# A linear-attention block with Strassen products: KV sums and numerators in PE array tiles, later exps, a third Strassen value pair

## Chip, cores, metric

One core of one Trainium2 chip. The metric is the time of one execution in microseconds (us) on the device, the median of several; smaller is better. All outputs were compared with the reference and were correct. All runs here are fast runs with a granted clock of 0.998 to 1.0.

## The reference, cut

```python
h  = x + A(layernorm(x))            # linear attention, 32 heads of 32
h2 = h + B(layernorm(h))            # gated feed-forward, F = 3584
# A, with S = 2048, D = 1024:
q, k, v = split_heads(x @ wqkv)
phi = lambda t: where(t > 0, t + 1, exp(t)) + 1e-6
kv  = einsum("bhsd,bhse->bhde", phi(k), v);  z = phi(k).sum(over s)
num = einsum("bhqd,bhde->bhqe", phi(q), kv)
den = einsum("bhqd,bhd->bhq", phi(q), z) + 1e-6
return (num / den) @ wo
```

Everything is bf16. The sum `z` is had by a column of ones beside `v`, the denominator by a column of `z` beside `kv`.

## The kernel before

The kernel writes each engine's instructions in a fixed order; every engine works through its own list in order, and a semaphore wait stands only where two engines meet. So *where in the program* an instruction stands decides what it blocks. The parts that matter (cuts marked):

**A Strassen group** makes a 2x2 block product from seven products of four 128x512 matmuls each. A product adds up in a *bank*, one of the eight 128x512 parts of the accumulator `ps`; a bank must be read out before another product takes it. They keep Strassen-like names but run in the order P1, P7, P6, P2, P5, P4, P3. In this text "the second product" means P2, and so on. After each, `hook(i)` runs work queued for that place. The exps of two of a group's four blocks are queued in this way: they are *deferred* into the next group.

```python
a = alloc_bank(pool); f = alloc_bank(pool); b = alloc_bank(pool)
prod(a, X(0,0), W(0,0), True, "P1")
ident_act(bank(b), bank(a), ...)          # "fk1": ACT copies the partial sum; P6 adds onto it
hook(1)
prod(f, SX(2), TW(2), True, "P7")         # SX, TW: operand sums made by DVE
ident_act(s7, bank(f), ...)
hook(2)
c = alloc_bank(pool)
prod(b, SX(1), TW(1), False, "P6")
ident_act(bank(c), bank(b), ...)          # "fk2": P5 adds onto it
hook(3)
prod(a, X(1,0), W(1,0), False, "P2");  # ... evacuate block 11 (for k and q: exp, min/add, max = phi)
hook(4)
prod(c, SX(0), TW(0), False, "P5")
ident_act(sc, bank(c), ...)               # "sc": must be read before P3 adds onto bank c
s22 = e22(bank(f), ..., sc, ...); s22[0]()    # DVE add, frees bank f
hook(5)
prod(b, X(1,1), TW(3), False, "P4")
s21 = e21(bank(b), ..., s7, ...); s21[0]()    # DVE add, frees bank b
hook(6)
prod(c, SX(3), W(1,1), False, "P3")
# ... what is left of the evacuation runs in the NEXT group's hooks:
pend[1] = s12
pend[2] = list(s22[1:])                   # exp on ACT, then two DVE operations
pend[3] = list(s21[1:])
hook(7)
```

**The order of groups**: eight plain value pieces of 8 matmuls, then key group 0, then four more plain value pieces (the third pair, row blocks 4 and 5), then key group 1, value group 3, key group 2, value group 4 and so on to key group 7; eight query groups (r = 0, 1; ct = 0 to 3); then the output projection, interleaved with the numerators; then the feed-forward part.

**KV sums and numerators**, one 128x128 product for four heads of which only the four diagonal 32x32 blocks are wanted:

```python
def kvacc(st):                            # 8 matmuls; bursts of two row blocks = 16
    for g in range(NG):                   # g: group of four heads, three PSUM banks
        mm(kv_out(g), pa[:, g*P:(g+1)*P], vv[:, sv, g, 0:P+1], first, ...)
# once: DVE multiplies by a block mask into kvz (5 operations)
def a2_num(st):                           # 8 matmuls, two per bank
    for g in range(NG):
        mm(ps[:, NB[g//2], (g%2)*256 : ...+P+HPG], pqT[:, r, t, g, i*P:(i+1)*P], kvz[:, g, 0:P+HPG], True, True, ...)
```

Five banks serve the groups (`P1_POOL = [3..7]`), four in the second row of query groups (`A_POOL[1] = [4..7]`).

Of the kernel before, what the change touches and what calls it, by code (L numbers as in the profile page):

```python
# [132 lines left out]
def bass_sequential_preLN__linear_attn_block__glu_gated_reglu__prompt_kernel(  # L133
# [17 lines left out]
    H = 32  # L151
# [20 lines left out]
    VW = P + 2  # L172
    KZW = P + HPG
    GPB = 3
    GPN = NW // P
# [22 lines left out]
    with es:  # L198
# [53 lines left out]
        RE = sb("RE", [P, NX1 * D + NPK * D + NV * NG * VW], bf16)  # L252
# [4 lines left out]
        vv = RE[:, o0:o0 + NV * NG * VW].rearrange("p (a g w) -> p a g w", a=NV, g=NG)  # L257
# [58 lines left out]
        ip_i = hsb[:, 0, 512:768].bitcast(dt.int32)  # L316
        jp_i = hsb[:, 0, 768:1024].bitcast(dt.int32)

        ident = sb("ident", [P, P], bf16)
        bmask = sb("bmask", [P, P], f32)  # L320
        bmask4 = sb("bmask4", [P, HPG], f32)
# [9 lines left out]
        zsb = sb("zsb", [P, NG], f32)  # L331
        kvz = sb("kvz", [P, NG, KZW], bf16)

# [45 lines left out]
        B_at = _Buf("at")  # L379
        B_bt = bufs("bt_", 2)  # L380
# [4 lines left out]
        B_kvz = bufs("kvz_", NG)  # L385
        B_zsb = _Buf("zsb")
# [35 lines left out]
        B_bmask = _Buf("bmask")  # L422
        B_bmask4 = _Buf("bmask4")
# [4 lines left out]
        B_ipi = _Buf("ipi")  # L428
        B_jpi = _Buf("jpi")
# [39 lines left out]
        B_TWq[3].over = [B_zeros, B_ipi, B_jpi]  # L469
        for b_ in B_hs:  # L470
            b_.over = [B_zeros, B_ipi, B_jpi, B_TWq[3], B_at]
# [10 lines left out]
        def alloc_bank(pool):  # L482
            b = min(pool, key=lambda b: bank_last[b])
            touch_bank(b)
            return b
# [11 lines left out]
        LOG2DH = Dh.bit_length() - 1  # L497
        PL.add("pool", lambda e: e.iota(ip_i, pattern=[[0, P]], base=0, channel_multiplier=1),
               writes=[B_ipi], name="iota_p")
        PL.add("pool", lambda e: e.iota(jp_i, pattern=[[1, P]], base=0, channel_multiplier=0),  # L500
               writes=[B_jpi], name="iota_j")
        PL.add("dve", lambda e: e.tensor_scalar(out=ip_i, in0=ip_i, scalar1=LOG2DH, scalar2=None,
                                                op0=ALU.arith_shift_right),
               reads=[B_ipi], writes=[B_ipi], name="shr_p")
        PL.add("dve", lambda e: e.tensor_tensor(out=bmask4[:], in0=ip_i[:, 0:HPG], in1=jp_i[:, 0:HPG],
                                                op=ALU.is_equal),
               reads=[B_ipi, B_jpi], writes=[B_bmask4], name="bmask4")
        PL.add("dve", lambda e: e.tensor_scalar(out=jp_i, in0=jp_i, scalar1=LOG2DH, scalar2=None,
                                                op0=ALU.arith_shift_right),
               reads=[B_jpi], writes=[B_jpi], name="shr_j")  # L510
        PL.add("dve", lambda e: e.tensor_tensor(out=bmask[:], in0=ip_i, in1=jp_i, op=ALU.is_equal),
               reads=[B_ipi, B_jpi], writes=[B_bmask], name="bmask")
        PL.add("pool", lambda e: e.memset(vv[:, :, :, P:VW], 1.0), writes=[B_vones], name="vones")
# [186 lines left out]
        KVB = [0, 1, 2]  # L700
        P1_POOL = [3, 4, 5, 6, 7]

        def kv_out(g, w=P + 1):
            c0 = (g % GPB) * KZW
            return ps[:, KVB[g // GPB], c0:c0 + w]

# [36 lines left out]
        def T1(st):  # L743
# [6 lines left out]
            for hf in range(2):  # L750
                PL.add("act", lambda e, hf=hf: e.activation(
                    out=xnT[:, hf * HDC:(hf + 1) * HDC, st * P:(st + 1) * P],
                    in_=tb[:, hf * HDC:(hf + 1) * HDC, :], func=ACTF.Identity),
                       reads=[B_bank[b]], writes=[B_xnT[st][hf]], name="evT1_%d_%d" % (st, hf))

# [26 lines left out]
        def v_out(st, j):  # L782
            return vv[:, st % NV, j * GPN:(j + 1) * GPN, 0:P]

        def gw(ap):
            return ap.rearrange("p (g w) -> p g w", w=P)
# [46 lines left out]
        def sgroup(pool, tok_major, X, SX, W, TW, e11, e12, e21, e22, name, hooks=(), isq=False):  # L833
# [21 lines left out]
            b = alloc_bank(pool)  # L855
# [6 lines left out]
            sc, bc = btmp[:, 0, :], B_bt[0]  # L862
            ident_act(s7, bank(f), [B_bank[f]], [b7], name + "s7")
            hook(2)
            c = alloc_bank(pool)
# [21 lines left out]
            pend[2] = list(s22[1:])  # L887
            pend[3] = list(s21[1:])
# [111 lines left out]
        kv_started = [False] * 8  # L1000

        def kvacc(st):
            sv = st % NV
            pa = pk_ap(st)
            for g in range(NG):
                half = (g * P) // NW
                kb = KVB[g // GPB]
                first = not kv_started[kb]
                kv_started[kb] = True
                mm(kv_out(g), pa[:, g * P:(g + 1) * P], vv[:, sv, g, 0:P + 1],  # L1010
                   first, st == NST - 1, [B_pk[pk_slot(st)][half], B_v[sv][half], B_vones], B_bank[kb],
                   "kvacc_%d_%d" % (st, g), skip=True)

        def kvfin():
            for b_ in KVB:
                touch_bank(b_)
            rb = [B_bank[b_] for b_ in KVB]
            for b0, nb, ng, g0 in ((0, 2, GPB, 0), (2, 1, NG - 2 * GPB, 2 * GPB)):
                src = ps[:, b0:b0 + nb, 0:ng * KZW].rearrange("p b (g w) -> p b g w", w=KZW)
                n = nb * ng  # L1020
# [627 lines left out]
```

## Time and profile before

| | us |
|---|---|
| median of 4 runs | 748.17 (747.94 to 748.42) |
| span in the profile | 746.0 |
| TensorE (PE) busy | 736.1, 99% |
| VectorE (DVE) busy | 536.7, 72% |
| ScalarE (ACT) busy | 309.7, 42% |
| from the end of the attention part to the end | 233.3 to 746 |

From the page: the engines (busy us, share of the span, instructions), and the chain that ended last.

```profile
PE 736.1 (99%) x3539; PEld 336.0 (45%) x3595; DVE 536.7 (72%) x1071; ACT 309.7 (42%) x536; POOL 43.9 (6%) x90
...
PE 88%; DVE 5%; ACT 4%; issue 2%; DMA 0%; SPq 0%; DVEq 0%; POOL 0%; ACTq 0%; POOLq 0%
```

TensorE is the bound: what matters is how many slots its products take and how long it stands between them. A busy share of 99% hides the second part: a matmul lasts 379 ns in the trace while the next starts 215 ns after it, so the record still counts as busy when the next product starts some 100 ns late. A product of four such matmuls starts 0.86 us after the one before it when nothing holds it.

The groups by shape, busy us and mean ns: numerators and KV sums of the kernel before.

```profile
L616 PE MATMUL ps<-kvz,RAB 128*128 128x132 bf16 x128 | 10.1, 221 | 0.0
L616 PE MATMUL ps<-RE 128*128 128x129 bf16 x128 | 9.0, 220 | 0.1
```

The timeline of TensorE in value group 4 (start us, length us, operation, count). The lines are P1 (P7 and P6 are cut), then P2, P5, P4 and the KV burst.

```profile
57.08 1.03 PE L616 MATMUL ps<-RAB 128*128 128x512 bf16 x4
...
59.78 1.03 PE L616 MATMUL ps<-RAB 128*128 128x512 bf16 x4
60.91 1.04 PE L616 MATMUL ps<-RW,RWG 128*128 128x512 f16 x4
61.78 1.03 PE L616 MATMUL ps<-RW,RAB 128*128 128x512 f16 x4
62.65 1.10 PE L616 MATMUL ps<-RE 128*128 128x129 bf16 x16
```

The KV burst starts at once (62.65, 0.87 after P4).

The second-row query group q12 (P1, P7, P6, P2, P5). `L903` are the adds of the group before.

```profile
158.42 1.03 PE L616 MATMUL ps<-RAB,RO 128*128 128x512 bf16 x4
159.28 1.03 PE L616 MATMUL ps<-RWG,RX 128*128 128x512 f16 x4
160.18 1.04 PE L616 MATMUL ps<-RWG,RH 128*128 128x512 f16 x4
161.06 1.03 PE L616 MATMUL ps<-RAB,RO 128*128 128x512 bf16 x4
162.07 1.04 PE L616 MATMUL ps<-RWG,RH 128*128 128x512 f16 x4
```

```profile
158.00 1.28 DVE L903 TENSOR_TENSOR RX<-ps,RX 128x512 f32<-128x512 f32 x2
```

The only large gap is 0.15 us behind P2. P5 waits for the second copy (fk2), which stands on ACT behind a deferred exp (`L684`):

```profile
160.90 0.62 ACT L684 ACTIVATE RX<-RX 128x512 bf16<-128x512 f32 x1
161.42 0.59 ACT L621 ACTIVATE ps<-ps 128x512 f32<-128x512 f32 x1
```

### The profile page before, as it was taken

To read this page: it belongs to the slowest core of one execution; us is meant where nothing else is said; L and a number is where in the kernel's file an instruction comes from. 1 tells how busy PE (TensorE), PEld (TensorE's weight loads), DVE (VectorE), ACT (ScalarE), POOL (GpSimd) and SP (SyncE) were. 2 spreads that over 40 slices of the span, in tenths; PEclk is the share of its full clock that TensorE was granted. 3 is DMA by queue.
4 is the path that set the end of the run, shared out by engine and by line. 5 is a ranking of instruction groups with operands and counts; after the bars stand their busy time and mean duration, and the time that the engine had idled before them with its cause. 6 is when DMAs were issued, how large, how long until landed. Compare 5 with 4: busy or idle time off the path is not lost.

```text
span 746.0 us, 10031 instructions
## 1 busy us (share of the span) xinstructions
PE 736.1 (99%) x3539; PEld 336.0 (45%) x3595; DVE 536.7 (72%) x1071; ACT 309.7 (42%) x536; POOL 43.9 (6%) x90
## 2 busy tenths in 40 slices
PE   9999999999999999999999999999999999999998
PEld 4444444344554444444444444444444444444443
DVE  7788866898775899787877585766867677563343
ACT  4767656665832354544543100035444454520000
POOL 2411000001350000000000010000000000000000
PEclk9999999999999999999999999999999999999999
DMA  9642144023998797666428899742324242036764
GB/s 305 202 103 68 35 135 156 1 29 84 230 223 248 222 278 210 179 176 171 142 85 253 231 254 305 240 121 77 110 61 112 58 113 56 1 85 184 211 189 135
DMA packets 160226, 113.38 MB, mean 152 GB/s; under 512 B 51505, under 2 KB 141361, under 8 KB 160177
## 3 DMA queue, kind: packets, MB, share of 16 engines
q1 hardware_dynamic: 160176, 112.75, 54.1%
q8 instruction: 28, 0.46, 0.3%
q14 instruction: 22, 0.17, 0.1%
HBM read 85.46 MB, written 15.73 MB: 136 GB/s over the span
## 4 chain that ended last, share of the span: by engine, by line
PE 88%; DVE 5%; ACT 4%; issue 2%; DMA 0%; SPq 0%; DVEq 0%; POOL 0%; ACTq 0%; POOLq 0%
PE ps L616 88%; DVE RAB L691 1%; ACT ps L621 1%; ACT RX L684 1%; DVE RE L1058 1%; DVE RX L688 1%; ACT RXH L654 1%; ACT RXH L659 1%; ACT RX L621 1%; DVE RX L903 0%; DMA RW<-in_B_W_down_dram 0%; SPq L522 0%; DVE RXH L1082 0%; PE ps L748 0%; DVE RE L691 0%
## 5 line engine op out<-in xcount | busy, mean ns | idle before, releaser
L621 ACT ACTIVATE ps<-ps 128x512 f32<-128x512 f32 x154 | 89.8, 584 | 180.2 <-PE ps L616 161.5
L616 PE MATMUL ps<-RC,RO 128*128 128x512 f16 x672 | 154.4, 379 | 0.5 <-DVE RE L1239 0.4
L616 PE MATMUL ps<-RW,RAB 128*128 128x512 f16 (+1 forms) x681 | 150.1, 379 | 0.6
L616 PEld LDWEIGHTS ps<-RW,RAB 128*128 128x128 bf16 (+1 forms) x692 | 67.7, 98 | 81.6
L616 PE MATMUL ps<-RH,RWG 128*128 128x512 bf16 x435 | 103.2, 379 | 1.0 <-DVE RAB L1232 0.3
L621 ACT ACTIVATE RE<-ps 128x512 f32<-128x512 f32 x120 | 70.8, 597 | 75.3 <-PE ps L616 52.8
L616 PEld LDWEIGHTS ps<-RC,RO 128*128 128x128 f16 x672 | 65.5, 98 | 80.5 <-ACT ps L621 1.1
L616 PE MATMUL ps<-RC,RWG 128*128 128x512 f16 x320 | 76.6, 379 | 0.1
L616 PEld LDWEIGHTS ps<-RH,RWG 128*128 128x128 bf16 x448 | 43.8, 98 | 53.4 <-DVE RAB L1232 0.8
L1232 DVE TENSOR_TENSOR RAB<-ps,RAB 128x512 bf16<-128x512 f32 x28 | 19.3, 690 | 63.6 <-PE ps L616 63.6
L621 ACT ACTIVATE RAB<-ps 128x512 bf16<-128x512 f32 x56 | 33.4, 597 | 61.9 <-PE ps L616 61.8
L616 PE MATMUL ps<-RH,RO 128*128 128x512 bf16 (+1 forms) x242 | 58.3, 379 | 0.7
L616 PE MATMUL ps<-RW,RE 128*128 128x512 bf16 x248 | 56.8, 379 | 0.8 <-DVE RXH L1082 0.4
L616 PE MATMUL ps<-RAB 128*128 128x512 bf16 x196 | 47.7, 379 | 0.3
L616 PEld LDWEIGHTS ps<-RC,RWG 128*128 128x128 bf16 (+1 forms) x320 | 30.0, 98 | 39.9 <-ACT ps L621 5.9
L1163 DVE TENSOR_TENSOR RO<-RWG,RO 128x512 f16<-128x512 bf16 x108 | 45.4, 420 | 1.8
L1163 DVE TENSOR_TENSOR RO<-RWG 128x512 f16<-128x512 bf16 x108 | 40.7, 418 | 3.2 <-DMA RWG<-in_B_W_up_dram 1.6
L1239 DVE TENSOR_TENSOR RE<-ps,RE 128x512 f32<-128x512 f32 x56 | 38.3, 690 | 4.9 <-ACT RE L621 4.9
L1244 DVE TENSOR_TENSOR RE<-ps,RE 128x512 f32<-128x512 f32 x56 | 38.1, 681 | 0.0
L616 PEld LDWEIGHTS ps<-RH,RO 128*128 128x128 f16 (+1 forms) x256 | 24.6, 98 | 29.4 <-ACT RX L621 1.1
L616 PEld LDWEIGHTS ps<-RW,RE 128*128 128x128 bf16 x256 | 24.5, 98 | 27.9 <-DVE RXH L1082 0.7
L688 DVE TENSOR_SCALAR RX<-RX 128x512 bf16<-128x512 bf16 x64 | 18.6, 290 | 22.8 <-ACT RX L684 22.7
(118 smaller groups left out, 764.8 us busy)
## 6 DMA issues: line engine op xcount, KB each, us to landing
RWG<-in_B_W_gate_dram SPq DMA_DIRECT2D x28, 512.0 KB, 4.0
RWG<-in_B_W_up_dram SPq DMA_DIRECT2D x28, 512.0 KB, 5.1
RW<-t_scr SPq DMA_DIRECT2D x56, 256.0 KB, 3.3
RW<-in_B_W_down_dram SPq DMA_DIRECT2D x42, 256.0 KB, 4.0
RW<-in_B_W_down_dram SPq DMA_DIRECT2D x14, 512.0 KB, 4.1
t_scr<-RW SPq DMA_DIRECT2D x14, 512.0 KB, 5.0
RE<-in_A_x_dram SPq DMA_DIRECT2D x23, 256.0 KB, 3.2
RAB<-in_A_wqkv_dram SPq DMA_DIRECT2D x8, 512.0 KB, 8.0
```

What stands on the lines that cost most here:

```text
L616: lambda e: e.matmul(out_ap, lhsT, rhs, start=start, stop=stop, skip_group_check=skip),
L621: PL.add("act", lambda e: e.activation(out=dst, in_=src, func=func), reads=reads, writes=writes, name=name)
L654: PL.add("act", lambda e: e.activation(out=junk, in_=src, func=ACTF.Identity, scale=1.0 / D, accum_out=sv[:, 0:1]), reads=src_bufs, writes ...
L659: PL.add("act", lambda e: e.activation(out=junk, in_=src, func=ACTF.Square, scale=float(D) ** -0.5, accum_out=sv[:, 1:2]), reads=src_bufs, ...
L684: PL.add("act", lambda e: e.activation(out=Et[:, k, :], in_=src, func=ACTF.Exp), reads=[src_buf], writes=[B_E[k]], name=name + "_exp")
L688: PL.add("dve", lambda e: e.tensor_scalar(out=Et[:, k, :], in0=Et[:, k, :], scalar1=1.0, scalar2=1e-6, op0=ALU.min, op1=ALU.add), reads=[] ...
L691: PL.add("dve", lambda e: e.scalar_tensor_tensor(out=dst_ap, in0=src, scalar=C1, in1=Et[:, k, :], op0=ALU.add, op1=ALU.max), reads=[src_bu ...
L1058: PL.add("dve", lambda e: e.tensor_tensor(out=osb[:, k, :].rearrange("p (g h e) -> p g h e", h=HPG, e=Dh), in0=nv[:, :, 0:P].rearrange("p ...
L1163: PL.add(eng, lambda e: e.tensor_tensor(out=Tring[:, k, j], in0=in0, in1=in1, op=ALU.subtract), reads=reads, writes=[B_T[k][j]], name="T%d ...
L1232: PL.add("dve", lambda e: e.tensor_tensor(out=hh[:, f1, 0:SBW], in0=bank(BA[1]), in1=r11[:, rr, :], op=ALU.mult), reads=[B_bank[BA[1]], B_ ...
L1239: PL.add("dve", lambda e, w=w: e.tensor_tensor(out=ftmp[:, 4 + w, :], in0=bank(BF_[w]), in1=ftmp[:, 2 + w, :], op=ALU.add), reads=[B_bank[ ...
L1244: PL.add("dve", lambda e, w=w: e.tensor_tensor(out=ftmp[:, 6 + w, :], in0=bank(BB[w]), in1=ftmp[:, w, :], op=ALU.add), reads=[B_bank[BB[w] ...
```

## The change

Its intent: fewer TensorE cycles and fewer TensorE waits in the attention part. (1) KV sums and numerators are computed per head in quarter-array tiles, so that only wanted blocks are computed and four small matmuls can run beside each other; the KV sums then fit one bank, masks go, two banks and some memory come free. (2) The two deferred exps of each group move one product later, out of the way of the copies; a second scratch tile for `sc`. (3) The third value pair becomes a Strassen group: 28 matmuls instead of 32. The core of the diff:

```diff
-        KVB = [0, 1, 2]
-        P1_POOL = [3, 4, 5, 6, 7]
+        KVB = 0
+        P1_POOL = [1, 2, 3, 4, 5, 6, 7]
@@ sgroup
-            sc, bc = btmp[:, 0, :], B_bt[0]
+            sc, bc = [(btmp[:, 0, :], B_bt[0]), (ctmp[:], B_ct)][grp[0] % 2]
-            pend[2] = list(s22[1:])
-            pend[3] = list(s21[1:])
+            pend[3] = list(s22[1:])
+            pend[4] = list(s21[1:])
@@ kvacc
-                mm(kv_out(g), pa[:, g * P:(g + 1) * P], vv[:, sv, g, 0:P + 1], first, ...
+                for h in range(HPG):
+                    c0 = g * P + h * Dh
+                    mm(ps[h * Dh:(h + 1) * Dh, KVB, g * VW:g * VW + Dh + 1], pa[:, c0:c0 + Dh],
+                       vv[:, sv, g * HPG + h, 0:Dh + 1], False, ...
@@ kvfin: five DVE operations become one ACT copy
@@ a2_num
-                mm(ps[:, nbk, c0:c0 + P + HPG], pqT[:, r, t, g, ...], kvz[:, g, 0:P + HPG], ...
+                for h in range(HPG):
+                    sl = slice(h * Dh, (h + 1) * Dh)
+                    mm(ps[:, NB[h], g * VW:g * VW + Dh + 1], pqT[sl, r, t, g, ...], kvz[sl, g, 0:Dh + 1], ...
@@ order of groups
-        k_group(0, ...); v_piece(4, 0, ...); v_piece(4, 1, ...); x_sums(1); v_piece(5, 0)
-        norms(3); twv.pop(0)(); v_piece(5, 1); x_sums(2); kvaccs(0)
-        for p in range(1, NP_):
+        for p in range(NP_):
@@ the last two KV bursts: hooks 5 and 6 -> hook 7
```

(Cut: layouts, masks, some small moves in the opening, the rule that keeps a bank last used for transposes from being chosen for a copied partial sum, A_POOL[0] with seven banks.)

More of the change, by code (lines that the diff above doesn't have):

```diff
@@ L171, in bass_sequential_preLN__linear_attn_block__glu_gated_reglu__prompt_kernel @@
     NKV = 2 * ND2
-    VW = P + 2
-    KZW = P + HPG
-    GPB = 3
-    GPN = NW // P
+    VW = Dh + 2
     NPASS = 2
@@ L250, in bass_sequential_preLN__linear_attn_block__glu_gated_reglu__prompt_kernel @@
         hnT = RH[:].rearrange("p (a b) -> p a b", a=NDC)
-        RE = sb("RE", [P, NX1 * D + NPK * D + NV * NG * VW], bf16)
+        RE = sb("RE", [P, NX1 * D + NPK * D + NV * H * VW], bf16)
         x1 = RE[:, 0:NX1 * D].rearrange("p (a b) -> p a b", a=NX1)
@@ L256, in bass_sequential_preLN__linear_attn_block__glu_gated_reglu__prompt_kernel @@
         o0 += NPK * D
-        vv = RE[:, o0:o0 + NV * NG * VW].rearrange("p (a g w) -> p a g w", a=NV, g=NG)
+        vv = RE[:, o0:o0 + NV * H * VW].rearrange("p (a h w) -> p a h w", a=NV, h=H)
         def pk_slot(st):
@@ L315, in bass_sequential_preLN__linear_attn_block__glu_gated_reglu__prompt_kernel @@
         zeros_t = hsb[:, 0, 0:512]
-        ip_i = hsb[:, 0, 512:768].bitcast(dt.int32)
-        jp_i = hsb[:, 0, 768:1024].bitcast(dt.int32)
+        ctmp = sb("ctmp", [P, NW], f32)
         ident = sb("ident", [P, P], bf16)
-        bmask = sb("bmask", [P, P], f32)
-        bmask4 = sb("bmask4", [P, HPG], f32)
         neghalf = sb("neghalf", [P, 1], f32)
@@ L330, in bass_sequential_preLN__linear_attn_block__glu_gated_reglu__prompt_kernel @@
         rden = sb("rden", [P, NDT, H], f32)
-        zsb = sb("zsb", [P, NG], f32)
-        kvz = sb("kvz", [P, NG, KZW], bf16)
+        kvz = sb("kvz", [P, NG, VW], bf16)
         ps = es.enter_context(nc.psum_tensor("ps", [P, 8, 512], f32))
@@ L379, in bass_sequential_preLN__linear_attn_block__glu_gated_reglu__prompt_kernel @@
         B_at = _Buf("at")
+        B_ct = _Buf("ct")
         B_bt = bufs("bt_", 2)
@@ L384, in bass_sequential_preLN__linear_attn_block__glu_gated_reglu__prompt_kernel @@
         B_E = bufs("E_", NPH)
-        B_kvz = bufs("kvz_", NG)
-        B_zsb = _Buf("zsb")
+        B_kvz = _Buf("kvz")
         B_pqT = [[bufs("pqT%d_%d_" % (r, t), NG) for t in range(2)] for r in range(2)]
@@ L421, in bass_sequential_preLN__linear_attn_block__glu_gated_reglu__prompt_kernel @@
         B_ident = _Buf("ident")
-        B_bmask = _Buf("bmask")
-        B_bmask4 = _Buf("bmask4")
         B_neghalf = _Buf("neghalf")
@@ L427, in bass_sequential_preLN__linear_attn_block__glu_gated_reglu__prompt_kernel @@
         B_vones = _Buf("vones")
-        B_ipi = _Buf("ipi")
-        B_jpi = _Buf("jpi")
         def flat(x):
@@ L468, in bass_sequential_preLN__linear_attn_block__glu_gated_reglu__prompt_kernel @@
             b_.over = flat(B_wkv)
-        B_TWq[3].over = [B_zeros, B_ipi, B_jpi]
+        B_TWq[3].over = [B_zeros]
         for b_ in B_hs:
-            b_.over = [B_zeros, B_ipi, B_jpi, B_TWq[3], B_at]
+            b_.over = [B_zeros, B_TWq[3], B_at]
         PL = _Plan()
@@ L480, in touch_bank, with alloc_bank @@
             bank_last[b] = bank_clock[0]
-        def alloc_bank(pool):
-            b = min(pool, key=lambda b: bank_last[b])
+        partial = set()
+        def alloc_bank(pool, copied=False):
+            b = min((b for b in pool if not (copied and b in partial)), key=lambda b: bank_last[b])
+            if not copied:
+                partial.discard(b)
             touch_bank(b)
@@ L496, in bass_sequential_preLN__linear_attn_block__glu_gated_reglu__prompt_kernel @@
         )
-        LOG2DH = Dh.bit_length() - 1
-        PL.add("pool", lambda e: e.iota(ip_i, pattern=[[0, P]], base=0, channel_multiplier=1),
-               writes=[B_ipi], name="iota_p")
-        PL.add("pool", lambda e: e.iota(jp_i, pattern=[[1, P]], base=0, channel_multiplier=0),
-               writes=[B_jpi], name="iota_j")
-        PL.add("dve", lambda e: e.tensor_scalar(out=ip_i, in0=ip_i, scalar1=LOG2DH, scalar2=None,
-                                                op0=ALU.arith_shift_right),
-               reads=[B_ipi], writes=[B_ipi], name="shr_p")
-        PL.add("dve", lambda e: e.tensor_tensor(out=bmask4[:], in0=ip_i[:, 0:HPG], in1=jp_i[:, 0:HPG],
-                                                op=ALU.is_equal),
-               reads=[B_ipi, B_jpi], writes=[B_bmask4], name="bmask4")
-        PL.add("dve", lambda e: e.tensor_scalar(out=jp_i, in0=jp_i, scalar1=LOG2DH, scalar2=None,
-                                                op0=ALU.arith_shift_right),
-               reads=[B_jpi], writes=[B_jpi], name="shr_j")
-        PL.add("dve", lambda e: e.tensor_tensor(out=bmask[:], in0=ip_i, in1=jp_i, op=ALU.is_equal),
-               reads=[B_ipi, B_jpi], writes=[B_bmask], name="bmask")
-        PL.add("pool", lambda e: e.memset(vv[:, :, :, P:VW], 1.0), writes=[B_vones], name="vones")
+        PL.add("pool", lambda e: e.memset(vv[:, :, :, Dh:VW], 1.0), writes=[B_vones], name="vones")
         PL.add("pool", lambda e: e.memset(neghalf[:], -0.5), writes=[B_neghalf], name="neghalf")
@@ L698, in phi @@
                 f_()
-        KVB = [0, 1, 2]
-        P1_POOL = [3, 4, 5, 6, 7]
-        def kv_out(g, w=P + 1):
-            c0 = (g % GPB) * KZW
-            return ps[:, KVB[g // GPB], c0:c0 + w]
+        KVB = 0
+        P1_POOL = [1, 2, 3, 4, 5, 6, 7]
         def run(ops, n):
@@ L754, in T1 @@
                        reads=[B_bank[b]], writes=[B_xnT[st][hf]], name="evT1_%d_%d" % (st, hf))
+            partial.add(b)
         def T1d(st):
@@ L782, in v_out @@
         def v_out(st, j):
-            return vv[:, st % NV, j * GPN:(j + 1) * GPN, 0:P]
+            return vv[:, st % NV, j * (H // 2):(j + 1) * (H // 2), 0:Dh]
         def gw(ap):
-            return ap.rearrange("p (g w) -> p g w", w=P)
+            return ap.rearrange("p (g w) -> p g w", w=Dh)
         def v_copy(b, st, j):
@@ L854, in sgroup @@
             f = alloc_bank(pool)
-            b = alloc_bank(pool)
+            b = alloc_bank(pool, True)
             prod(a, X(0, 0), W(0, 0), True, "P1")
@@ L861, in sgroup @@
             s7, b7 = [(atmp, B_at), (btmp[:, 1, :], B_bt[1])][grp[0] % 2]
-            sc, bc = btmp[:, 0, :], B_bt[0]
+            sc, bc = [(btmp[:, 0, :], B_bt[0]), (ctmp[:], B_ct)][grp[0] % 2]
             ident_act(s7, bank(f), [B_bank[f]], [b7], name + "s7")
             hook(2)
-            c = alloc_bank(pool)
+            c = alloc_bank(pool, True)
             prod(b, SX(1), TW(1), False, "P6")
@@ L998, in q_group @@
                    add_phi(*dst(1, 1), "q_%d_%d" % (r, ct)), "q%d%d" % (r, ct), hooks, True)
-        kv_started = [False] * 8
         def kvacc(st):
@@ L1006, in kvacc @@
                 half = (g * P) // NW
-                kb = KVB[g // GPB]
-                first = not kv_started[kb]
-                kv_started[kb] = True
-                mm(kv_out(g), pa[:, g * P:(g + 1) * P], vv[:, sv, g, 0:P + 1],
-                   first, st == NST - 1, [B_pk[pk_slot(st)][half], B_v[sv][half], B_vones], B_bank[kb],
-                   "kvacc_%d_%d" % (st, g), skip=True)
-        def kvfin():
-            for b_ in KVB:
-                touch_bank(b_)
-            rb = [B_bank[b_] for b_ in KVB]
-            for b0, nb, ng, g0 in ((0, 2, GPB, 0), (2, 1, NG - 2 * GPB, 2 * GPB)):
-                src = ps[:, b0:b0 + nb, 0:ng * KZW].rearrange("p b (g w) -> p b g w", w=KZW)
-                n = nb * ng
-                PL.add("dve", lambda e, src=src, g0=g0, n=n, nb=nb, ng=ng: e.tensor_tensor(
-                    out=kvz[:, g0:g0 + n, 0:P].rearrange("p (b g) w -> p b g w", b=nb), in0=src[:, :, :, 0:P],
-                    in1=bmask[:].unsqueeze(1).unsqueeze(1).to_broadcast([P, nb, ng, P]), op=ALU.mult),
-                       reads=rb + [B_bmask], writes=B_kvz[g0:g0 + n], name="kvm_%d" % g0)
-                PL.add("dve", lambda e, src=src, g0=g0, n=n, nb=nb, ng=ng: e.tensor_copy(
-                    out=zsb[:, g0:g0 + n].rearrange("p (b g) -> p b g", b=nb), in_=src[:, :, :, P]),
-                       reads=rb, writes=[B_zsb], name="zsb_%d" % g0)
-            PL.add("dve", lambda e: e.tensor_tensor(
-                out=kvz[:, :, P:P + HPG], in0=bmask4[:].unsqueeze(1).to_broadcast([P, NG, HPG]),
-                in1=zsb[:].unsqueeze(2).to_broadcast([P, NG, HPG]), op=ALU.mult),
-                   reads=[B_zsb, B_bmask4], writes=B_kvz, name="zc")
@@ L1033, in bass_sequential_preLN__linear_attn_block__glu_gated_reglu__prompt_kernel @@
-        A_POOL = [[3, 4, 5, 6, 7], [4, 5, 6, 7]]
+                for h in range(HPG):
+                    c0 = g * P + h * Dh
+                    mm(ps[h * Dh:(h + 1) * Dh, KVB, g * VW:g * VW + Dh + 1], pa[:, c0:c0 + Dh],
+                       vv[:, sv, g * HPG + h, 0:Dh + 1], False, st == NST - 1,
+                       [B_pk[pk_slot(st)][half], B_v[sv][half], B_vones], B_bank[KVB], "kvacc_%d_%d" % (st, g),
+                       skip=True)
+        def kvfin():
+            touch_bank(KVB)
+            PL.add("act", lambda e: e.activation(
+                out=kvz[:, :, 0:Dh + 1], in_=ps[:, KVB, 0:NG * VW].rearrange("p (g w) -> p g w", w=VW)[:, :, 0:Dh + 1],
+                func=ACTF.Identity), reads=[B_bank[KVB]], writes=[B_kvz], name="kvz")
@@ L1035, in bass_sequential_preLN__linear_attn_block__glu_gated_reglu__prompt_kernel @@
+        A_POOL = [[1, 2, 3, 4, 5, 6, 7], [4, 5, 6, 7]]
         NB = [0, 1, 2, 3]
@@ L1041, in a2_num @@
             for g in range(NG):
-                nbk = NB[g // 2]
-                c0 = (g % 2) * 256
-                mm(ps[:, nbk, c0:c0 + P + HPG], pqT[:, r, t, g, i * P:(i + 1) * P], kvz[:, g, 0:P + HPG],
-                   True, True, [B_pqT[r][t][g], B_kvz[g]], B_bank[nbk], "num_%d_%d" % (st, g))
+                for h in range(HPG):
+                    sl = slice(h * Dh, (h + 1) * Dh)
+                    mm(ps[:, NB[h], g * VW:g * VW + Dh + 1], pqT[sl, r, t, g, i * P:(i + 1) * P],
+                       kvz[sl, g, 0:Dh + 1], True, True, [B_pqT[r][t][g], B_kvz], B_bank[NB[h]],
+                       "num_%d_%d" % (st, g), skip=True)
         def a2_div(st):
@@ L1051, in a2_div @@
             rb = [B_bank[b_] for b_ in NB]
-            nv = ps[:, 0:4, :].rearrange("p b (g w) -> p (b g) w", w=256)
+            nv = ps[:, 0:HPG, 0:NG * VW].rearrange("p h (g w) -> p g h w", w=VW)
             PL.add("dve", lambda e: e.tensor_scalar(
-                out=dtmp[:, kd, :].rearrange("p (g h) -> p g h", h=HPG), in0=nv[:, :, P:P + HPG],
+                out=dtmp[:, kd, :].rearrange("p (g h) -> p g h", h=HPG), in0=nv[:, :, :, Dh],
                 scalar1=1e-6, scalar2=None, op0=ALU.add), reads=rb, writes=[B_dt[kd]], name="dtmp_%d" % st)
@@ L1059, in a2_div @@
                 out=osb[:, k, :].rearrange("p (g h e) -> p g h e", h=HPG, e=Dh),
-                in0=nv[:, :, 0:P].rearrange("p g (h e) -> p g h e", e=Dh),
+                in0=nv[:, :, :, 0:Dh],
                 in1=rden[:, kd, :].rearrange("p (g h) -> p g h", h=HPG).unsqueeze(3).to_broadcast([P, NG, HPG, Dh]),
@@ L1404, in bass_sequential_preLN__linear_attn_block__glu_gated_reglu__prompt_kernel @@
         load_wkv(3)
-        pe_dummies(12, P1_POOL)
+        pe_dummies(12, [KVB] + P1_POOL)
         s0, s1_, s2_, s3 = [ln1_steps(st) for st in range(4)]
@@ L1412, in bass_sequential_preLN__linear_attn_block__glu_gated_reglu__prompt_kernel @@
         T1(0)
-        pe_dummies(3, [alloc_bank(P1_POOL)])
+        pe_dummies(3, P1_POOL[-1:])
         for f_ in s1_[1:] + s2_[:1]:
@@ L1439, in bass_sequential_preLN__linear_attn_block__glu_gated_reglu__prompt_kernel @@
         v_piece(3, 0)
+        ln1_stats(4)
         q5()
-        ln1_stats(4)
         twk.pop(0)()
@@ L1454, in bass_sequential_preLN__linear_attn_block__glu_gated_reglu__prompt_kernel @@
         twk.pop(0)()
+        twv.pop(0)()
         twv.pop(0)()
@@ L1480, in k6 @@
                     f_()
-                if 3 <= p + 2 < NP_:
+                if p + 2 < NP_:
                     x_sums(p + 2)
@@ L1493, in kvaccs @@
             kvacc(2 * p + 1)
-        k_group(0, kv_hooks(0, (0, 0)))
-        def run_pend(i):
-            for f_ in pend.pop(i, ()):
-                f_()
-        v_piece(4, 0, lambda: run_pend(1))
-        run_pend(2)
-        v_piece(4, 1, lambda: run_pend(3))
-        x_sums(1)
-        v_piece(5, 0)
-        norms(3)
-        twv.pop(0)()
-        v_piece(5, 1)
-        x_sums(2)
-        kvaccs(0)
         NQ = {2: (0, 1), 3: (0, 1), 4: (0, 1), 5: (2, 2), 6: (1, 0)}
-        for p in range(1, NP_):
+        for p in range(NP_):
             nq = NQ.get(p, (0, 0))
@@ L1514, in bass_sequential_preLN__linear_attn_block__glu_gated_reglu__prompt_kernel @@
             if p == NP_ - 1:
-                hooks[5] = lambda h5=hooks[5]: (h5(), kvaccs(NP_ - 2))
+                hooks[7] = lambda: kvaccs(NP_ - 2)
             k_group(p, hooks)
@@ L1518, in v6 @@
                 def v6(p=p, nq=nq):
+                    if p == 0:
+                        x_sums(1)
                     norms(p + 3)
@@ L1531, in bass_sequential_preLN__linear_attn_block__glu_gated_reglu__prompt_kernel @@
                 if r == 0 and ct == 0:
-                    hooks[6] = lambda: kvaccs(NP_ - 1)
+                    hooks[7] = lambda: kvaccs(NP_ - 1)
                 if r == 0 and ct == 2:
```

## The prediction

> **What bounds the kernel now.** TensorE. The page has PE busy 736.1 of 746.0 us (99%), DVE 72%, ACT 42%; the chain that ended last is 88% PE. Only TensorE slots and TensorE waits count. The change touches only about the first 230 us.
>
> **What changes, costed from the trace.**
>
> 1. *KV sums and numerators.* The groups by shape show 128 KV matmuls (128x129) and 128 numerator matmuls (128x132). In the timeline 16 KV matmuls start 58.5 ns apart (89.76 to 90.64 us), 8 numerator matmuls 58.6 ns apart: together 256 x 58.5 ns = 15.0 us. The change makes each into four small ones (33 columns, a quarter of the array): 1024 matmuls, 1024 weight loads. Two outcomes:
>    - The four overlap. The Trainium skill, "TensorE: Matmul & The Clock Gate", gives about 4 ns between starts on different tiles (Part 3) and a start-to-start floor of about 25 ns for small matmuls (Part 1). Estimate from that page: 25 to 30 ns per set of four, so 15.0 becomes about 7.5 us. No run here shows it yet.
>    - They (or their weight loads) go one by one at that floor: 100 ns per set, +10.6 us.
>    - Either way "TensorEngine Tiling (Array Packing)", Key Properties, says a change of tiling mode drains the array. A 512-column matmul lasts 379 ns against 215 ns between starts, so a drain costs up to an estimated 160 ns. 8 KV bursts (16 sets) and 16 numerator bursts (8 sets) make 48 switches: up to 7.7 us, most of the gain.
> 2. *Third value pair by Strassen.* 32 matmuls become 28: -4 x 215 ns = -0.9 us. Its operand sums come late on DVE; I expect 0.3 to 1 us of wait once, near 30 us.
> 3. *Later exps, second scratch tile.* Gaps between matmul starts show that copies on ACT hold the next product: 147 ns between second and fifth product in most query groups, 99 + 47 ns in most value groups, and a repeated 34 ns that is the copy itself and stays. Moving the exps behind the copies should save about 0.9 us in query groups, 0.5 us elsewhere. Against it: a key group's last phi comes later, and the KV burst in the next value group may wait 0.1 to 0.4 us for it, 6 times.
> 4. *One KV bank, one ACT copy in place of five DVE operations, no mask set-up.* Off the chain. More free banks are worth little: the gaps are not bank waits.
>
> **Sum.** Items 2 to 4: about -1.5 us. Item 1: -7 to 0 if tiles overlap (about 2 in 3), +11 to +18 if not. I predict 746 us, 738 to 764 for 8 in 10; faster by over 2% 0.03, within 2% 0.86, slower by over 2% 0.11.
>
> **What would show each step.** Start-to-start of small matmuls: about 7 ns if they overlap, 25 if not; length of a KV burst (0.93 us now) and of a numerator burst (0.46 us now); an extra gap of up to 160 ns at both edges if the switch drains. Gap between second and fifth product of query groups: 147 down to about 34 ns. TensorE waits for DVE near 30 us and before KV bursts. Feed-forward passes of unchanged length.
>
> **What would make it wrong.** Weight loads of 32 columns that are not hidden, which would make a set cost far more than 100 ns; a switch that does not drain, some 8 us more gain; the later phi holding up KV bursts; more TensorE instructions slowing the instruction supply.

## The result

The time after is 750.47 us, median of 4 (749.90 to 751.02), against 748.17 before. The ratio is 1.0031, 95% interval 1.0013 to 1.0048. A ratio is the mean time of one kernel's fast runs over that of the other's fast runs of the same rounds, so it is not quite the ratio of the medians quoted beside it. The change is inside the predicted range and within 2%, but it has the other sign than the likely case of the prediction: a small loss.

The page after, the same lines, and TensorE's waits by releaser (us in total, times, longest).

```profile
PE 731.2 (98%) x4298; PEld 326.2 (44%) x4359; DVE 534.3 (71%) x1064; ACT 310.8 (41%) x539; POOL 42.6 (6%) x88
...
PE 84%; DVE 8%; ACT 3%; issue 3%; DMA 1%; SPq 0%; DVEq 0%; ACTq 0%
```

```profile
L594 PE MATMUL ps<-RE 128*32 128x33 bf16 x512 | 6.0, 179 | 2.4 <-DVE RE L669 2.3
L594 PE MATMUL ps<-kvz,RAB 32*128 32x33 bf16 x512 | 5.9, 174 | 0.5 <-DVE RE L1021 0.5
```

```profile
PE ps L594 <- DVE RE L669: 2.3, 6, 0.4
PE ps L594 <- DVE RWG L800: 2.2, 2, 1.8
```

The tiled work shrank from 19.1 us of busy records to 11.9, while the chain went from 88 to 84% PE and from 5 to 8% DVE: TensorE now waits for DVE, by this count 2.3 us for a phi before KV matmuls (six times) and 2.2 us for operand sums (twice).

**Numerators.** A burst of 32 small matmuls between two big products:

```profile
151.73 0.59 PE L594 MATMUL ps<-RAB,RXH 128*128 128x512 bf16 x2
152.25 0.37 PE L594 MATMUL ps<-kvz,RAB 32*128 32x33 bf16 x32
152.56 0.39 PE L594 MATMUL ps<-RH,RO 128*128 128x512 f16 x1
```

All 32 start within 0.2 us. A *set* is the four small matmuls of one group of four heads, one in each tile. In the single records the four of a set start 2 to 4 ns apart, and sets 25 ns apart (39 from the first to the second). The last big matmul starts at 151.943 and would give way at 152.159 (0.216 later); the first small one starts at 152.255: 96 ns of nothing. The last small one starts at 152.453 and the next big one 104 ns later. These two stretches are called the *edges* of a burst. So the burst costs 0.398 us, edges included, against 0.470 before.

**Value group 4 with its KV burst**, to be read beside the lines of before:

```profile
58.97 1.03 PE L594 MATMUL ps<-RAB 128*128 128x512 bf16 x4
...
61.67 1.03 PE L594 MATMUL ps<-RAB 128*128 128x512 bf16 x4
62.57 1.04 PE L594 MATMUL ps<-RW,RWG 128*128 128x512 f16 x4
63.45 1.03 PE L594 MATMUL ps<-RW,RAB 128*128 128x512 f16 x4
64.40 0.38 PE L594 MATMUL ps<-RE 128*32 128x33 bf16 x32
65.16 0.38 PE L594 MATMUL ps<-RE 128*32 128x33 bf16 x32 [0.39 <-DVE RE L669]
```

P2 to P5 is 0.90 us, down from 1.13: the later exps did what they were meant to. But the second half of the burst starts at 65.16 instead of about 64.6: it needs the phi of the key group's last block, whose exp now comes a product later. The 0.5 us lost here is more than the 0.23 won above.

**Query group q12**, TensorE, and then DVE and ACT in its beginning:

```profile
160.45 1.03 PE L594 MATMUL ps<-RAB,RO 128*128 128x512 bf16 x4
161.48 1.04 PE L594 MATMUL ps<-RWG,RX 128*128 128x512 f16 x4
162.69 1.04 PE L594 MATMUL ps<-RWG,RH 128*128 128x512 f16 x4 [0.18 <-ACT ps L599]
163.57 1.03 PE L594 MATMUL ps<-RAB,RO 128*128 128x512 bf16 x4
164.46 1.04 PE L594 MATMUL ps<-RWG,RH 128*128 128x512 f16 x4
```

```profile
160.13 0.69 DVE L669 SCALAR_TENSOR_TENSOR RAB<-RX 128x512 bf16<-128x512 f32 x1
160.74 0.68 DVE L878 TENSOR_TENSOR RX<-ps,RX 128x512 f32<-128x512 f32 x1
161.34 0.68 DVE L878 TENSOR_TENSOR RXH<-ps,RXH 128x512 f32<-128x512 f32 x1
```

```profile
162.06 0.58 ACT L599 ACTIVATE ps<-ps 128x512 f32<-128x512 f32 x1 [0.81 <-DVE RXH L878]
```

P2 to P5 is now 0.89 us (1.01 before), but P1 to P7 takes 1.03 and P7 to P6 1.21 (0.86 and 0.90 before). The phi operations of the later exps stand ahead of the adds that free banks f and b: before, these began at 158.00, 0.42 us ahead of P1; now at 160.74, 0.29 behind it. P7 needs bank f, and ACT's copy into bank b waits 0.81 us for the second add. This row has four banks, so that there is no other bank to take: in the first row, with seven banks, the same order of work shows neither gap (0.87 and 0.90 us in q01).

**Third and fourth value group** (value groups 2 and 3 by number): P1 and P7 in each, and what DVE waited for.

```profile
29.79 1.03 PE L594 MATMUL ps<-RAB 128*128 128x512 bf16 x4
31.19 1.04 PE L594 MATMUL ps<-RW,RWG 128*128 128x512 f16 x4 [0.38 <-DVE RWG L800]
...
43.68 1.03 PE L594 MATMUL ps<-RAB 128*128 128x512 bf16 x4
46.48 1.26 PE L594 MATMUL ps<-RW,RWG 128*128 128x512 f16 x5 [1.77 <-DVE RWG L800]
```

```profile
46.00 0.76 DVE L800 TENSOR_TENSOR RWG<-RAB 128x512 f16<-128x512 bf16 x2 [1.86 <-DMA RAB<-RXH]
```

P7 starts 0.54 and 1.94 us late, since it needs DVE's operand sums. In the fourth group these wait for the DMA transpose of its rows, whose norms moved to the end of the third group.

**Where the time went, by stage.** Every matmul has a weight-load record (3595 before, 4359 after), and the weights of the next matmul start loading 1 to 2 ns after a matmul starts (11 ns where that matmul had waited), so the start of every product is known even where a matmul record is missing. Sums of start-to-start times in us; an edge ahead of a burst counts to the stage before it. The last three columns belong to experiments below.

| stage | before | after | tiles_only | after_early | best2 |
|---|---|---|---|---|---|
| opening, key group 0, third value pair | 35.04 | 35.16 | 35.71 | 35.57 | 34.56 |
| KV bursts (8) | 7.77 | 7.99 | 5.39 | 5.10 | 7.31 |
| key groups 1 to 7 | 43.50 | 42.97 | 43.60 | 43.18 | 43.63 |
| value groups 3 to 7 | 32.04 | 33.23 | 32.58 | 33.72 | 31.37 |
| query groups, first row | 25.28 | 25.59 | 25.34 | 25.16 | 25.22 |
| query groups, second row | 24.98 | 26.97 | 25.40 | 25.41 | 25.41 |
| numerators (16) | 8.07 | 6.24 | 5.97 | 5.88 | 5.65 |
| output projection | 55.24 | 57.15 | 56.73 | 56.59 | 56.58 |
| feed-forward | 508.84 | 508.77 | 509.25 | 508.75 | 508.97 |
| sum | 740.76 | 744.07 | 739.97 | 739.36 | 738.70 |

The sums differ by +3.31 from before to after, as the spans do (746.0, 749.3). Each column is one execution, and that of after is the slowest of its four (751.02 us): by the medians the difference is 2.30. The opening (up to key group 0) varies between 21.8 and 22.6 us over all the profiles (no run settles why), the first feed-forward pass between 170.5 and 171.3; so a difference of half a microsecond in these two rows means nothing.

### The profile page after: what moved, and what is told of

It is laid out like the page before. It is cut to its first block, busy times and chain, and to the rows that moved or that the text cites. A ratio compares the mean times of both kernels' runs of the same rounds, so it can differ in the third digit from the quotient of the medians.

```text
span 749.3 us, 11528 instructions
## 1 busy us (share of the span) xinstructions
PE 731.2 (98%) x4298; PEld 326.2 (44%) x4359; DVE 534.3 (71%) x1064; ACT 310.8 (41%) x539; POOL 42.6 (6%) x88
## 4 chain that ended last, share of the span: by engine, by line
PE 84%; DVE 8%; ACT 3%; issue 3%; DMA 1%; SPq 0%; DVEq 0%; ACTq 0%
PE ps L594 84%; ACT ps L599 2%; DVE RE L669 1%; ACT RX L662 1%; DVE RAB L669 1%; DVE RX L666 1%; DMA RE<-in_A_x_dram 1%; DMA RAB<-RXH 1%; DVE RX L878 0%; SPq L500 0%; DVE RW L775 0%; DMA RW<-in_B_W_down_dram 0%; DVE RXH L1045 0%; PE ps L722 0%; DVE RXH L878 0%
## 5 line engine op out<-in xcount | busy, mean ns | idle before, releaser
L594 PE MATMUL ps<-RH,RWG 128*128 128x512 bf16 x448 | 106.0, 379 | 0.2 <-DVE RAB L1195 0.2
L594 PE MATMUL ps<-RH,RO 128*128 128x512 bf16 (+1 forms) x228 | 55.5, 379 | 1.9
L594 PE MATMUL ps<-RAB 128*128 128x512 bf16 x173 | 42.6, 379 | 0.3
```

The lines of the kernel that those rows point to most:

```text
L594: lambda e: e.matmul(out_ap, lhsT, rhs, start=start, stop=stop, skip_group_check=skip),
```

## The experiments

Two theories stood at the start. A: the tiles gain and the new order of work loses. B: the tiles are a wash, eaten by mode switches, and the waits are theirs. Twelve kernels ran; ratios are to the kernel before in the same rounds, whose median was 747.6 to 748.2. Kernels of different rounds are best compared by their ratios.

| run | median us | ratio | 95% interval |
|---|---|---|---|
| after | 750.47 | 1.0031 | 1.0013 to 1.0048 |
| tiles_only | 746.32 | 0.9978 | 0.9964 to 0.9992 |
| before_late | 754.97 | 1.0097 | 1.0083 to 1.0111 |
| after_qearly | 748.24 | 1.0009 | 0.9997 to 1.0022 |
| after_kv7 | 750.46 | 1.0038 | 1.0026 to 1.0051 |
| after_early | 746.36 | 0.9984 | 0.9970 to 0.9997 |
| after_sums | 750.04 | 1.0033 | 1.0020 to 1.0047 |
| after_no3rd | 749.35 | 1.0021 | 1.0007 to 1.0035 |
| tiles_split | 746.83 | 0.9990 | 0.9977 to 1.0004 |
| best2 | 745.55 | 0.9971 | 0.9958 to 0.9985 |
| best3 | 745.98 | 0.9976 | 0.9964 to 0.9989 |
| before_exp3 | 748.99 | 1.0018 | 1.0005 to 1.0031 |
| best4 | 749.79 | 1.0024 | 1.0010 to 1.0037 |

### tiles_only: the tiles on the old order of work

The hunks of the tiles alone, on the kernel before (in short; the first line is against the kernel before, the two of the banks against the kernel after):

```diff
+  KV sums in four column tiles, one bank; numerators in four row tiles; one ACT copy for kvz
-        KVB = 0;  P1_POOL = [1, 2, 3, 4, 5, 6, 7];  A_POOL[0] = [1, ..., 7]
+        KVB = 0;  P1_POOL = [3, 4, 5, 6, 7];        A_POOL[0] = [3, ..., 7]
   (exps, single scratch tile, plain third pair, hooks as before)
```

> The kernel before with only the KV sums and numerators in array tiles (its own order of work, its five-bank pool, its plain value pieces). Theory A (the tiles gain, the new order of work loses): a numerator burst with its two edges goes from 0.47 to 0.40 us, 16 times, -1.1 us; a KV burst from 0.94 to about 0.60 us, 8 times, -2.7 us; since this order has the phi ready when the KV burst starts, there is no wait inside it. Expect 744 to 745 us, ratio to before about 0.995. Rival B (the tiles are a wash or a loss: the switches of tiling mode eat what they save): 748 us or more, and the KV bursts with edges no shorter than 0.85 us.

746.32 us, 0.9978: a gain, about 1.6 us. Theory A by its sign; the size was less than half of what I expected. The numerator bursts came as said (0.398 us). A KV burst costs 0.730 with both edges, not 0.60. The records say why: the first eight sets start 25 ns apart, later ones mostly 33 to 37 ns, with the small matmuls 8 to 9 ns apart instead of 3 (see tiles_split).

### before_late: the later exps on the kernel before

```diff
-            pend[2] = list(s22[1:])
-            pend[3] = list(s21[1:])
+            pend[3] = list(s22[1:])
+            pend[4] = list(s21[1:])
```

(and the same in the plain value pieces after key group 0.)

> The kernel before with only the two deferred exps of each Strassen group moved one product later (one scratch tile as before: a second does not fit beside the masks). Theory A: value groups lose the 265 ns wait between second and fifth product (6 to 7 times, about -1.4 us), but query groups get a wait between fourth and third product (about 0.27 us, first row of groups) and waits before seventh and sixth product (0.17 + 0.35 us, second row), and KV bursts wait 0.4 to 0.5 us for the last phi, 6 times: +2 to +3.5 us in all, 750 to 752 us. Rival B (the later exps help, as they were meant to): 746 to 747 us.

754.97 us, 1.0097: a loss of 7.3 us, over twice what I expected. One line of the waits:

```profile
PE ps L616 <- DVE RE L691: 4.2, 7, 1.9
```

By stages: KV bursts 12.87 us instead of 7.77, query groups 52.65 instead of 50.26; value groups 3 to 7 won 1.13. My expectation was too small because the kernel before has its last two bursts one or two products earlier than the kernel after, which makes the phi later still for them (1.9 us for one).

### after_qearly: exps early in the query groups alone

```diff
-            pend[3] = list(s22[1:])
-            pend[4] = list(s21[1:])
+            pend[2 if isq else 3] = list(s22[1:])
+            pend[3 if isq else 4] = list(s21[1:])
```

> The kernel after with the exps back in their earlier places in the query groups alone. Theory A: the four second-row query groups fall from 7.0 to about 6.65 us each with their numerator burst, the first row from 6.38 to 6.3, and the stall of 0.7 + 0.8 us at the start of the output projection shrinks: -1.5 to -2.5 us, 748 to 749 us. Rival B (the query waits come from the tiles, for instance from the numerator's four banks or the mode switch): unchanged at 750.5 us, with the 0.17 and 0.35 us gaps still there.

748.24 us, 1.0009, about 1.6 us better than after by the ratios. Second-row groups are back to 6.35 us (6.71 to 6.82 in after), and the 0.17 and 0.35 us gaps are gone: theory A; the tiles do not make these waits.

### after_kv7: the KV bursts one product later

```diff
-                    kvaccs(p)                       # in hook 6, ahead of P3
-                v_group(p + 2, {6: v6})
+                v_group(p + 2, {6: v6, 7: lambda p=p: kvaccs(p)})
```

> The kernel after with each KV burst one product later (after the last product of the value group instead of before it). Theory A (the KV burst waits for the last phi of the key group, 0.53 us, 6 times): the wait inside the burst goes, burst with edges 0.60 us, -3 us, 747 to 748 us. Rival B (the 0.55 us gap in the middle of the burst belongs to the tiles, for example to the change of the stationary block or to instruction supply): the gap moves with the burst, time unchanged at 750.5 us.

750.46 us: no change, yet rival B is not the reason. The bursts did lose their wait (5.34 us for eight instead of 7.99). In value group 6 (P4, P3, burst):

```profile
90.66 1.03 PE L594 MATMUL ps<-RW,RAB 128*128 128x512 f16 x4
91.82 1.04 PE L594 MATMUL ps<-RAB,RH 128*128 128x512 bf16 x4
92.78 0.70 PE L594 MATMUL ps<-RE 128*32 128x33 bf16 x64
```

P4 to P3 is now 1.16 us instead of 0.86. P3 adds onto the bank that ACT still copies (`sc`), late because a deferred exp stands ahead of it. That wait had been hidden under the KV burst. With some 0.8 us more of wait for operand sums in value groups 4 and 5, all 2.7 us came back elsewhere. A wait taken away is worth only what the next one leaves.

### after_early: exps early everywhere

```diff
-            pend[3] = list(s22[1:])
-            pend[4] = list(s21[1:])
+            pend[2] = list(s22[1:])
+            pend[3] = list(s21[1:])
```

> The kernel after with the exps back in their earlier places in all groups; second scratch tile, seven banks, tiles and the third Strassen value pair stay. Theory A (the later exps are the part that loses): against after_qearly (748.2) the KV bursts lose their 0.53 us wait six times (-3.2 us), the value groups get back their 265 ns wait five or six times (+1.4 us): 746 to 747 us. Rival B (the wait in the KV burst is not the exps' doing): KV bursts still 1.08 us long, 749 us or more.

746.36 us, 0.9984: as theory A said. KV bursts fall to 5.10 us, the query groups to 50.57 from 52.56, and value groups 4 to 7 get their wait of 0.26 us behind P2 back. P1, P7 and P6 of a second-row query group (q11), with the tiles still in:

```profile
157.41 1.03 PE L594 MATMUL ps<-RAB,RO 128*128 128x512 bf16 x4
158.27 1.03 PE L594 MATMUL ps<-RWG,RX 128*128 128x512 f16 x4
159.17 1.04 PE L594 MATMUL ps<-RWG,RH 128*128 128x512 f16 x4
```

The starts are 0.86 and 0.90 us apart, as in the kernel before. The later exps alone cost the change about 3.5 us (1.0031 against 0.9984 of 748), more than its whole loss.

### after_sums and after_no3rd: the third value pair

```diff
 after_sums
+   key group 0: x_sums(2) in hook 4 instead of 6;   value group 2: norms(3) in hook 3 instead of 6
 after_no3rd
+   plain v_piece(4, 0), (4, 1), (5, 0), (5, 1) after key group 0, as before,
+   with norms(3), the operand sums and the first KV burst in their old places
```

> The kernel after with two things moved to an earlier place: the operand sums of the third pair two products earlier, and the norms of row blocks 6 and 7 (whose transposes the fourth pair's sums wait for) three products earlier. Theory A (the third Strassen pair saves its 0.86 us but pays 0.5 + 1.9 us because these come late): both stalls, before the seventh product of the third and of the fourth value group, go: -2.4 us, about 748 us. Rival B (the transposes are late for another reason, the DMA queue): the 1.9 us stall stays.

> The kernel after with the third value pair in plain pieces again (as before). Theory A: four more matmuls (+0.86 us) but neither the 0.5 nor the 1.9 us stall: -1.5 us, about 749 us. Rival B (the pair is a gain, the stalls would be elsewhere without it): +0.9 us, 751.4 us.

after_no3rd: 749.35, 1.0021, 0.8 us better than after by the ratios. The intervals overlap, so the totals do not show a gain; the stages show that the 0.5 and 1.9 us stalls are gone. As the pair stands, with the places that came with it, no saving shows. after_sums: 750.04, 1.0033: no gain, though both stalls went (value groups 2 and 3: 14.88 us down to 12.61). KV bursts took 0.76 us of it: DVE now runs the norms ahead of the phis of key group 0, and the first burst waits 1.2 us for those. Its profile has a span 1.1 us shorter, the medians do not show it. So: the stalls' cause is shown, this way to mend them is not a gain. Without its stall the pair does save: value group 2 takes 6.29 us (start to start, without its KV burst) against 7.00 for the plain pieces in after_no3rd.

### tiles_split: why a KV burst is slower per set

On tiles_only, five bursts cut in two halves with P3 between:

```diff
-                    kvaccs(p)                       # 64 small matmuls in hook 6
+                    kvacc(2 * p)                    # 32 in hook 6
+                v_group(p + 2, {6: v6, 7: lambda p=p: kvacc(2 * p + 1)})
```

> tiles_only with five of the KV bursts cut into two halves of 32 small matmuls, a product of four big matmuls between them: five more pairs of mode switches, the same work. Theory Q (the first 64 instructions of a burst come out of the full queue, 25 ns for a set of four; later ones come at the rate of supply, 34 ns for a set): both halves run at 25 ns, so a half with edges takes 0.40 us, two 0.80 against 0.73 for the whole burst, +0.07 us five times, +0.35 us in all. Rival D (a set of four takes about 33 ns in a KV burst anyway, for instance for the column tiles' weight loads; only the switches count, 0.19 us each pair): +1 us, and sets beyond the eighth at 34 ns in both halves.

TensorE in one value group (half, P3, half, next P1):

```profile
62.17 0.38 PE L589 MATMUL ps<-RE 128*32 128x33 bf16 x32
62.48 1.04 PE L589 MATMUL ps<-RAB,RH 128*128 128x512 bf16 x4
63.44 0.38 PE L589 MATMUL ps<-RE 128*32 128x33 bf16 x32
63.75 0.39 PE L589 MATMUL ps<-RAB 128*128 128x512 bf16 x1
```

Each half costs 0.401 or 0.402 us with edges, all sets but the first 25 ns apart: theory Q to the nanosecond, five more pairs of switches for 0.07 us each (median 746.83; 0.9 us above tiles_only by the ratios, within the intervals). So the slower second half of a whole burst is not the column tiles' own; it begins with the 33rd matmul, the 65th instruction counting weight loads. The kernel after shows the same without a cut: where its burst stands 0.56 us at the 33rd matmul for a phi, the sets behind start 25 ns apart again. The Trainium skill, "TensorE: Matmul & The Clock Gate" (Part 1), gives the queue of TensorE as 64 deep; the place where the slowing begins agrees with it. That the supply of instructions is what limits the rest (34 ns for eight instructions) is the reading; no run measured the supply by itself, and none cut a burst at another length.

### before_exp3, best2, best3, best4: mending the change

```diff
 before_exp3 (on before) and best2 (on after)
+            pend[2 if isq else 3] = list(s22[1:])
+            pend.setdefault(3, []).extend(s21[1:])   # both directly behind fk2
 best2 also
+   x_sums(2) in hook 4 of key group 0; norms(3) in hook 4 of value group 2
 best3 = best2 with
-   stats(0); first half of stats(1); norm(0)
+   stats(0); norm(0); first half of stats(1)
 best4 = best2 with
+   KV bursts in hook 7;  evacuation of block 11 queued behind the sc copy (key and value groups, q00)
```

> The kernel before (no tiles, five banks) with the same placing of the exps as best2 and nothing else. Theory A (what the later exps were meant to gain is there, they only went one product too far): value groups lose 0.23 us of wait each, six or seven times, KV bursts still without a wait of more than 0.1 us: -1.4 us, 746.3 us. Rival B (moving the exps brings nothing without the tiles' freed banks and scratch): 747.6 us or more.

before_exp3: 748.99, 1.0018, a small loss: rival B. Value groups won 1.13 us (0.26 us behind P2 became 0.03), but KV bursts cost 10.64 instead of 7.77. The second exp has the same place in ACT's list as before, but the first now stands directly ahead of it: in value group 4 it starts 0.30 us later and its DVE work, behind that of the first, 0.72 us later. That is enough: the KV burst is the deadline, and the old order just met it.

> The kernel after, mended in three places: in key groups both deferred exps go directly behind the second copy of the next value group (one product later than before for the first exp, not later for the second), in query groups they are back in their earlier places; the third pair's operand sums go two products earlier; the norms of row blocks 6 and 7 two products earlier. KV bursts stay before the last product. Theory A: against after_early (746.4) the value groups lose the 265 ns wait (-0.23 us six or seven times) without a new wait in the KV burst (burst 0.64 us after its first edge), and the stalls at the third and fourth value pair (0.8 + 1.4 us) go: 743 to 744.5 us, ratio to before about 0.995. Rival B (DVE is the limit here, so each wait taken away comes back at another place): 746 us.

best2: 745.55, 0.9971: the lowest median here, 2.2 us under before and 4.5 under after by the ratios (its interval overlaps those of best3, after_early and tiles_only). Value groups 31.37 us, third pair without its stall; KV bursts still wait about 0.3 us each (1.9 us for phis in its waits), and P7 of key group 1 now starts 0.41 us late; together about what is missing to the 743 to 744.5 expected.

> best2 with the first row block's norm placed on DVE ahead of the second block's first statistics, so that the first transposes no longer wait behind a statistic whose input's DMA lands late: the opening up to the first key group goes to about 22.0 us in the profile where other runs had 21.8 to 22.6. Theory A: -0.2 to -0.4 us against best2. Rival: the opening is bound by the weights' DMA, no change.

best3: 745.98, 0.9976; no gain over best2, its opening 22.36 us: the rival's outcome. Its reason, the weights' DMA, is not shown; in the waits 0.4 us are put down to it.

> best2 with each KV burst after the last product of its value group, and the evacuation of the first output block queued on ACT behind the fifth product's copy, so that this copy is in time for the last product. Theory A (in best2 the KV burst still waits about 0.3 us for the last phi, and where the burst is moved alone, as in after_kv7, the copy comes late instead; both can be had): KV bursts 0.64 us after the first edge with no wait, no wait of more than 0.05 us before the last product of value groups, -1.5 to -2.2 us against best2 (745.5), so 743.3 to 744 us. Rival B (DVE and ACT order give the time back in the next group, or in the feed-forward part's start): 745 us or more, with new waits before the seventh product or in the first feed-forward pass.

best4: 749.79, 1.0024: rival B. KV bursts fell to 5.09 us and P3 starts in time, but in value groups 3 to 7 P7 starts 1.33 us late. DVE ahead of that P7:

```profile
57.89 0.29 DVE L666 TENSOR_SCALAR RX<-RX 128x512 bf16<-128x512 bf16 x1 [2.85 <-ACT RX L662]
...
60.02 0.75 DVE L800 TENSOR_TENSOR RWG<-RAB 128x512 f16<-128x512 bf16 x2
```

DVE stands idle for 2.85 us for an exp that this run moved behind a copy on ACT, and the operand sums (`L800`) stand behind it in DVE's list: idle, but not free.

## Why the prediction was right or wrong

It gave 746 us with 738 to 764 and "within 2%" at 0.86; 750.47 is inside. That is partly luck: the range was so wide on account of tiles that might not overlap, and they did. Its likely case, a gain of some microseconds, did not come.

1. *Tiles overlap (held 2 in 3).* Right. Starts on different tiles are some 3 ns apart, against about 4 ns in the Trainium skill, "TensorE: Matmul & The Clock Gate" (Part 3), and a set of four takes 25 ns in a numerator burst. Edges were put at up to 160 ns each; 93 to 96 ahead of a burst and 104 to 110 from the last small start to the next big one were measured. That switches eat most of the gain held for the numerators: 0.470 to 0.398 with edges. A KV burst went from 0.94 to 0.73, of which 0.20 are edges. "-7 to 0" came out as about -1.6 us (tiles_only). KV sets beyond the eighth at 34 ns were not costed; the prediction names a slower instruction supply only as a risk.
2. *Third pair: -0.9 us and 0.3 to 1 us of wait once.* The first stall was in this range (0.54 us). The second, 1.94 us in the next value group by way of the norms and their transposes, was not foreseen. The loss of the pair as it stands, about 0.8 us by the ratios, is not clear of the noise; without the stalls value group 2 is shorter by the pair (6.29 us in after_sums against 7.00).
3. *Later exps: "about 0.9 us in query groups, 0.5 us elsewhere" of saving against 0.1 to 0.4 us of wait, six times.* This is the step that failed, and it gave the sum its wrong sign: the term is +3.5 us (after against after_early), not the gain or near-zero that I took it for. Its parts: the saving in value groups was 0.23 us each, larger than the "99 + 47" says, because I took 216 ns of a 263 ns gap for a missing record; the wait in the KV burst was real and 0.53 us; and the query groups lost instead of winning, because I costed ACT alone. The gap that it named did close, from about 0.15 us to 0.03 behind P2, but 0.17 and 0.35 us came up before P7 and P6. The phi work of the moved exps is on DVE, ahead of the adds that free two of four banks.
4. *Masks and banks worth little.* Held, as far as seen: with seven banks and a second scratch tile, early exps, a key group takes 6.12 us against 6.19 (after_early, tiles_only).

"Feed-forward passes of unchanged length" held (508.84 and 508.77). Open: the output projection grew by 1.91 us, of which 12 x 0.096 = 1.15 are edges ahead of bursts; how much of the other 0.76 is due to the exps is not settled (after_early and after_qearly have it some 0.56 shorter, but waits for DMA vary there by as much).

## What to carry to other kernels

Splitting a product into array tiles saves only what is left after two edges of about 0.1 us for each burst, so make few bursts: here one burst of 64 small matmuls (0.73 us) was cheaper than two of 32 (0.80), though its second half ran slower. Before moving an operation on a busy engine, follow everything behind it in *each* engine's list to the next deadline: here an exp moved on ACT took DVE's adds, and with them PSUM banks, one product later. Read gaps from start times; a product that starts 0.26 us late shows no idle line while the records before it still run.

## What the Trainium skill lacked or had wrong

- "TensorEngine Tiling (Array Packing)", Key Properties: says that a switch of tiling mode drains, with no figure. Here 93 to 96 ns from the end of the last big matmul's slot to the first small start, and 104 to 110 ns from the last small start to the next big one; a burst of 32 small matmuls costs 0.40 us, of which 0.2 is work.
- "TensorE: Matmul & The Clock Gate", Part 1: "Start-to-start never drops below ≈25 ns however small N is" does not hold across tiles: starts are some 3 ns apart (its own Part 3 has about 4), and the 25 ns is the time of a whole set of four, one matmul in each tile.
- The same page has the 64-deep queue but not what follows: from the 65th instruction of a burst on, a set of four takes 33 to 37 ns in most cases instead of 25 (tiles_only; gone in tiles_split, and in after where the burst stands at its 33rd matmul).
